# A two-layer MLP on one core: W2's block sums moved in whole blocks

## The chip, the cores and the metric

The kernel runs on one core of a Trainium2 chip. The metric is the device time of one execution in microseconds (us). A core has five engines with instruction queues of their own: TensorE (PE; its weight loads are shown as PEld), VectorE (DVE), ScalarE (ACT), GpSimd (POOL) and SyncE (SP), which here issues nearly all DMA transfers. Each queue is worked through in order; engines wait for one another by semaphores.

## The reference

```python
B, S, D, F = 1, 2048, 1024, 3584

def reference(x, w1, b1, w2, b2):
    y = _layernorm(x, axis=-1)
    h = _gelu(jnp.einsum("bsd,df->bsf", y, w1) + b1)
    return jnp.einsum("bsf,fd->bsd", h, w2) + b2
```

All inputs and the output are bf16.

## The kernel before

Both products are done by a Winograd form of Strassen's scheme: a product of 2 x 2 blocks takes seven block products of sums of blocks instead of eight. The first product (y by W1) uses it once. The second (h by W2) uses it twice: an outer level with seven products p, and inside each an inner level with seven products q. `Wino.step(q)` runs the seven and combines them in PSUM: matmuls (L878 for the first product, L1135 for the second), copies by ACT (L804, L813) and additions by DVE (L821).

Tokens come in two blocks b of 1024. x is normalised by tiles of 128 tokens; block 0's tiles are transposed by PE, block 1's by DMA transposes (L676). W1 is loaded by seven chunks of 256 columns, once for each token block (`w1_load`, L717 and L722), and its block sums are made by DVE (`w1_sums`, L745). h stays in SBUF. GELU is L797.

W2's sums are made beside the first product by the class `W2Sums`. The outer level needs, of the four blocks B11, B12, B21, B22, the sums T1 to T4; each of seven operands (B11, T1, T3, B22, B21, T2, T4, for p = 1, 5, 7, 3, 2, 6, 4) then needs four inner sums (q = 5, 6, 7, 4). W2 is taken in four chunks of k (k0 to k1 of seven: two, two, two, one). A block's chunk is held as four quarter tiles (s for the half of rows, v for the half of columns) of n = (k1 - k0) x 512 bytes a partition. `load` (L916) issues a transfer per quarter, `outer` (L927) a subtraction per quarter, `inner` (L948) makes the four sums, and `store` (L936) writes every sum, and for T1 to T4 the three quarters that q = 1, 2, 3 use, to `w2_scr` in HBM, one transfer each. In the second product `w2_unit` reads one unit of 448 KB per (p, q): from `w2_scr` (L993), or for q = 1, 2, 3 of B11, B21, B22 from W2 itself (L991). The units are used by both token blocks and loaded for the first.

Quarters and sums live in a zone of SBUF of their own, MZ, of ZONE = 20 * 1024 - 192 bytes a partition. An allocation picks the place that was freed longest ago; its first writer waits for the last readers of what lay there, DMA stores included.

The order of the work is made in two layers. `flat` is a list of steps (group, q): 73 steps of token block 0 (A, from 0), 98 of block 1 (B, from 73), 98 of the second product (C, from 171). Loads, sums and stores are put at steps of this list; a DMA put at a step is held until the PE task before that step. W2_AT spreads the 14 parts of `W2Sums.steps()` over a range of steps for each of the four chunks, and Y1_AT and Y1_STEP place the loads and norms of block 1's x tiles. Then `schedule` simulates all engines with a duration for each task, takes among the ready tasks of an engine the one that is due first, and the order that comes out is the order of each queue on the chip. For a transfer it counts an issue time (0.1 us on SP), then the transfer at 360 GB/s behind the transfers before it, and a latency (`dma_lat`). Buffers are packed by the simulated times in six rounds, and the round with the shortest simulated span is used.

Of the kernel before, what the change touches and what calls it, by code (L numbers as in the profile page):

```python
# [13 lines left out]
P = 128  # L14
# [30 lines left out]
WAR = 0.5  # L45
SLACK = 4.0
ZONE = 20 * 1024 - 192
PACK_ROUNDS = 6


# [219 lines left out]
class Program:  # L270
# [25 lines left out]
        return t  # L296


    def schedule(self, pe_t0, rounds=0, dma_bw=0.36e6, dma_lat=1.9):
        tasks = self.tasks  # L300
        for t in tasks:
            t.succ = []
        for t in tasks:
            for d in t.deps:
                d.succ.append(t)
        pe = [t for t in tasks if t.eng == "PE"]
        at = pe_t0
# [19 lines left out]
    def _simulate(self, pe, dma_bw, dma_lat):  # L327
# [17 lines left out]
        while done < len(tasks):  # L345
            progressed = False
            for e in ENG:
                q = waiting[e]
                while q and q[0][0] <= now + 1e-9:
                    _, _, t = heapq.heappop(q)  # L350
                    heapq.heappush(heaps[e], (t.alap, t.i, t))
            for e in ENG:
                h = host.get(e, e)
                while free[h] <= now + 1e-9:
                    if e == "PE":
                        if pe_next >= len(pe):
                            break
                        t = pe[pe_next]
                        if left[t] or ready_at[t] > now + 1e-9:
                            break  # L360
                        pe_next += 1
                    else:
                        if not heaps[e]:
                            break
                        _, _, t = heapq.heappop(heaps[e])
                    t.start = now
                    if e in ("SP", "ACTQ", "POOLQ"):
                        issue = 0.1 if e == "SP" else 0.5
# [12 lines left out]
                    heapq.heappush(events, t.done)  # L381
                    for s in t.succ:
                        left[s] -= 1
                        fin = t.end if (s.eng == t.eng == "PE") else t.done
                        ready_at[s] = max(ready_at[s], fin)
                        if not left[s] and s.eng != "PE":
                            heapq.heappush(waiting[s.eng], (ready_at[s], s.i, s))
                    done += 1
                    progressed = True
            if progressed:  # L390
                continue
            while events and events[0] <= now + 1e-9:
# [89 lines left out]
HEAD_T = (2, 4, 6, 7)  # L482
ACT_LN = (8, 9, 10, 11, 12, 13, 14, 15)
UNIT_LA, IN_LA = 3, 6
W2_AT = ((0, 2, ("A", 14), ("A", 50)), (2, 4, ("A", 50), ("B", 4)), (4, 6, ("B", 5), ("B", 50)), (6, 7, ("B", 50), ("C", -20)))
S1_AT = -2
W2_K = 2
NACC = 5
Y1_AT, Y1_STEP = 0, 3
T_PE = 7.5  # L490

OPA = {1: "A11", 2: "A12", 3: "S4", 4: "A22", 5: "S1", 6: "S2", 7: "S3"}
# [8 lines left out]
def d_tt(n):  # L501
    return n / 1920 + 0.075


def bass_standalone__mixer_channel_mlp__prompt_kernel(
# [24 lines left out]

    NCHUNK = NR // 2
    w1_scr = nc.dram_tensor("w1_scr", (NCHUNK, P, 4 * KH * 256), F16).ap()
    w2_scr = nc.dram_tensor("w2_scr", (8, 8, P, KQ * NCOL), F16).ap()

    with ExitStack() as es:
        block = es.enter_context(nc.Block())
# [20 lines left out]
        def build(pr, M, MA, MZ):  # L557
# [343 lines left out]
            def w2_dt(nm):  # L901
                return BF16 if nm.startswith("B") else F16

            class W2Sums:


# [2 lines left out]
                    self.B = {}  # L909

                def load(self, nm):
                    n = self.n
                    for s in range(2):
                        for v in range(2):
                            bf = self.B[nm, s, v] = MZ.alloc(n, nm)
                            dma("SP", lambda e, s=s, v=v, bf=bf: e.dma_start(v3(bf, 0, n, self.k1 - self.k0, BF16),  # L916
                                                                      w2_src(JK[nm], (s, v))[:, self.k0:self.k1, :]),
                                [], [bf.c()], P * n, None, f"ld{nm}{s}{v}")

                def outer(self, dst, a, bb, place):  # L920

                    n = self.n
                    for s in range(2):
                        for v in range(2):
                            ba, b_, bp = (self.B[z, s, v] for z in (a, bb, place))
                            op("DVE", d_tt(n // 2),
                               lambda e, ba=ba, b_=b_, bp=bp: e.tensor_tensor(out=v16(bp), in0=v16(ba, 0, n, w2_dt(a)),  # L927
                                                                             in1=v16(b_, 0, n, w2_dt(bb)), op=ALU.subtract),
                               r=[ba.c(), b_.c()], w=[bp.c()], name=f"{dst}{s}{v}")
                            self.B[dst, s, v] = self.B.pop((place, s, v))  # L930

                def store(self, p, q, buf):
                    c = Cell()
                    scr2.setdefault((p, q), []).append(c)
                    lo, hi, n = self.k0 * NCOL, self.k1 * NCOL, self.n
                    dma("SP", lambda e: e.dma_start(w2_scr[p, q][:, lo:hi], v16(buf)), [buf.c()], [c], P * n, None, f"sp2_{p}{q}")  # L936

                def inner(self, p, nm):

                    n, dt = self.n, w2_dt(nm)  # L940
                    Y = {(s, v): (v16(self.B[nm, s, v], 0, n, dt), self.B[nm, s, v].c()) for s in range(2) for v in range(2)}
                    if not nm.startswith("B"):
                        for q, sv in QIN.items():
                            self.store(p, q, self.B[nm, sv[0], sv[1]])

                    def mk(q, a, bb):
                        t = MZ.alloc(n, f"w2t{q}")
                        op("DVE", d_tt(n // 2), lambda e: e.tensor_tensor(out=v16(t), in0=a[0], in1=bb[0], op=ALU.subtract),  # L948
                           r=[a[1], bb[1]], w=[t.c()], name=f"w2t{p}{q}")
                        self.store(p, q, t)  # L950
                        return t, (v16(t), t.c())
                    b1_, t1 = mk(5, Y[0, 1], Y[0, 0])
                    b2_, t2 = mk(6, Y[1, 1], t1)
                    MZ.free(b1_)
                    b3_, t3 = mk(7, Y[1, 1], Y[0, 1])
                    MZ.free(b3_)
                    b4_, t4 = mk(4, Y[1, 0], t2)
                    MZ.free(b2_)
                    MZ.free(b4_)

                def free(self, nm):
                    for s in range(2):
                        for v in range(2):
                            MZ.free(self.B.pop((nm, s, v)))

                def steps(self):
                    return [
# [475 lines left out]
```

## Time and profile before

| | us |
|---|---|
| median of 3 runs | 384.94 |
| lowest and highest run | 384.37, 389.06 |
| the profiled execution | 383.47 |
| its span, first to last instruction | 381.5 |
| PE, DVE, ACT, POOL busy | 342.4, 299.3, 185.7, 14.9 |

The profile is of one execution. In it, L878 and the like are lines of the kernel. A row of a group names engine, operation, output and input, shapes and count, then busy us, mean ns of one, and the idle time of the engine ahead of these instructions with what ended it. `mem` is the one large SBUF tensor, `ps` a PSUM bank, `w_scr` stands for both scratch tensors in HBM, `in_w_dram` for W1 and W2. SPq is SP's queue of transfers. The slices cut the span in 40 equal parts of 9.54 us; a digit is a busy share in tenths. The DMA share is the mean busy share of the core's 16 DMA engines, from their packets' times, and can come out a little over 1.

### The profile page before, as it was taken

How to read it: one execution, taken by the hardware profiler on the slowest of the kernel's cores; microseconds unless marked ns; L12 is line 12 of the kernel's file. 1: busy time of each engine (PE TensorE's matmuls, PEld its weight loads, DVE VectorE, ACT ScalarE, POOL GpSimd, SP SyncE). 2: the span in 40 equal slices, each digit the busy share in tenths (PEclk: the TensorE clock that was granted, in tenths of full speed). 3: DMA queues.
4: the chain of work that ended last, by engine and by line, in shares of the span. 5: the costliest groups of instructions: out<-in, count | busy, mean ns of one | idle time of the engine just before them, and what ended most of it. 6: DMA issues, size and time to landing. Idle time of an engine off the chain costs nothing.

```text
span 381.5 us, 6308 instructions
## 1 busy us (share of the span) xinstructions
PE 342.4 (90%) x2363; PEld 222.6 (58%) x2363; DVE 299.3 (78%) x541; ACT 185.7 (49%) x327; POOL 14.9 (4%) x32
## 2 busy tenths in 40 slices
PE   8899987997859996799495999999999999998993
PEld 6754432443314442344142478888888888887882
DVE  4976558896788967786757799998798987799762
ACT  2598977979747663474344853444311122211110
POOL 2220000202100000000000000000000000000000
PEclk9999998999999999699698999999999999999998
DMA  8931389899986898895855255446384655567532
GB/s 246 315 103 28 97 243 273 228 278 310 253 208 206 282 310 243 285 306 176 228 157 165 64 179 151 144 144 192 112 228 147 205 157 153 184 180 220 169 121 69
DMA packets 101527, 74.01 MB, mean 194 GB/s; under 512 B 14330, under 2 KB 94330, under 8 KB 101498
## 3 DMA queue, kind: packets, MB, share of 16 engines
q1 hardware_dynamic: 101354, 73.50, 66.0%
q8 instruction: 18, 0.29, 0.3%
q10 hardware_dynamic: 144, 0.13, 0.1%
q14 instruction: 11, 0.09, 0.1%
HBM read 48.96 MB, written 22.54 MB: 187 GB/s over the span
## 4 chain that ended last, share of the span: by engine, by line
PE 60%; DMA 25%; DVE 6%; SPq 5%; issue 3%; ACT 0%; DVEq 0%
PE ps L1135 34%; PE ps L878 23%; DMA mem<-in_w_dram 15%; DMA mem<-w_scr 4%; DMA mem<-in_x_dram 3%; DMA mem<-mem 3%; SPq L916 2%; DVE mem L948 2%; PE ps L1186 2%; SPq L936 2%; DVE ps L821 1%; DVE mem L745 1%; PE ps L662 1%; DVE mem L694 1%; DVE mem L927 1%
## 5 line engine op out<-in xcount | busy, mean ns | idle before, releaser
L878 PE MATMUL ps<-mem 128*128 128x512 f16 x756 | 174.3, 391 | 27.3 <-DMA mem<-in_w_dram 17.5
L1135 PE MATMUL ps<-mem 128*128 128x256 f16 (+1 forms) x1372 | 151.7, 273 | 3.6 <-DMA mem<-in_w_dram 1.4
L878 PEld LDWEIGHTS ps<-mem 128*128 128x128 f16 (+1 forms) x756 | 74.3, 100 | 123.9 <-DMA mem<-in_w_dram 20.0
L1135 PEld LDWEIGHTS ps<-mem 128*128 128x128 f16 x1372 | 133.4, 98 | 22.5 <-DMA mem<-w_scr 2.9
L813 ACT COPY mem<-ps 128x512 f32<-128x512 f32 x111 | 65.2, 593 | 82.0 <-PE ps L1135 67.7
L797 ACT ACTIVATE mem<-ps,b_sb 128x512 f16<-128x512 f32 x112 | 73.2, 699 | 44.2 <-DVE ps L821 35.5
L1039 DVE TENSOR_TENSOR mem<-mem 128x1792 f16<-128x1792 f16 x56 | 60.3, 1085 | 11.9 <-PE ps L1135 4.7
L821 DVE TENSOR_TENSOR ps<-ps,mem 128x512 f32<-128x512 f32 x84 | 58.3, 694 | 14.3 <-ACT mem L813 9.3
L745 DVE TENSOR_TENSOR mem<-mem 128x1024 f16<-128x1024 bf16 (+1 forms) x56 | 37.0, 687 | 18.3 <-DMA mem<-in_w_dram 18.3
L948 DVE TENSOR_TENSOR mem<-mem 128x512 f16<-128x512 f16 (+3 forms) x112 | 39.8, 385 | 10.3 <-DMA mem<-in_w_dram 7.7
L804 ACT COPY ps<-ps 128x512 f32<-128x512 f32 x31 | 17.9, 579 | 35.2 <-PE ps L1135 27.8
L1050 DVE TENSOR_TENSOR mem<-mem 128x1792 f16<-128x1792 f16 x32 | 33.8, 1086 | 0.7 <-PE ps L1135 0.6
L927 DVE TENSOR_TENSOR mem<-mem 128x512 f16<-128x512 bf16 (+1 forms) x64 | 23.8, 386 | 5.9 <-DMA mem<-in_w_dram 4.0
L1067 DVE TENSOR_TENSOR mem<-ps,mem 128x512 bf16<-128x512 f32 x24 | 16.3, 689 | 8.3 <-PE ps L1135 4.2
L1080 DVE TENSOR_TENSOR mem<-ps,mem 128x512 f32<-128x512 f32 x24 | 15.9, 683 | 0.9 <-DMA out_dram<-mem 0.9
L633 DVE BATCH_NORM_STATS2 st_sb<-mem 128x6 f32<-128x512 bf16 x16 | 10.4, 672 | 5.2 <-DMA mem<-in_x_dram 5.2
L667 ACT COPY mem<-ps 128x512 f16<-128x512 f16 x16 | 8.7, 603 | 10.4 <-PE ps L662 10.4
L694 DVE TENSOR_TENSOR mem<-mem 128x512 f16<-128x512 f16 x32 | 12.0, 420 | 1.5 <-DMA mem<-mem 1.4
L616 ACT ACTIVATE mem<-mem 128x1024 f16<-128x1024 bf16 x8 | 8.4, 1052 | 4.7 <-DMA mem<-in_x_dram 4.7
L619 ACT ACTIVATE mem<-mem,mv_sb 128x1024 f16<-128x1024 bf16 x8 | 9.3, 1167 | 0.0
L1156 PE MATMUL ps<-ones 128*128 128x128 bf16 (+1 forms) x58 | 7.4, 302 | 1.0 <-POOL nhalf L583 1.0
L1186 PE MATMUL ps<-mem 128*128 128x128 f16 x112 | 7.6, 219 | 0.3 <-ACT mem L667 0.2
(30 smaller groups left out, 71.8 us busy)
## 6 DMA issues: line engine op xcount, KB each, us to landing
mem<-w_scr SPq DMA_DIRECT2D x40, 448.0 KB, 3.5
w_scr<-mem SPq DMA_DIRECT2D x120, 128.0 KB, 3.1
mem<-in_w_dram SPq DMA_DIRECT2D x28, 256.0 KB, 5.0
mem<-in_w_dram SPq DMA_DIRECT2D x14, 512.0 KB, 4.4
mem<-in_w_dram SPq DMA_DIRECT2D x48, 128.0 KB, 3.2
out_dram<-mem SPq DMA_DIRECT2D x32, 128.0 KB, 2.2
mem<-in_w_dram SPq DMA_DIRECT2D x9, 448.0 KB, 4.1
mem<-in_x_dram SPq DMA_DIRECT2D x15, 256.0 KB, 4.7
```

Source lines behind the costliest of these rows:

```text
L745: op("DVE", d_tt(n), lambda e: e.tensor_tensor(out=o[0], in0=a[0], in1=bb[0], op=f), r=[a[1], bb[1]], w=[o[1]], name=f"w1S{k}_{ch}")
L797: op("ACT", A_GELU, lambda e: e.activation(out=dst, in_=bank2(bank), func=ACT.Gelu_apprx_tanh, bias=b1_sb[:, f:f + 1], scale=1.0), r=[bank ...
L804: op("ACT", A_CP, lambda e: e.copy(out=banks[dst][:, :], in_=banks[src][:, :]), r=[bank_c[src]], w=[bank_c[dst]], name=name, lat=A_LAT)
L813: op("ACT", A_CP, lambda e: e.copy(out=v16(a, 0, 2048, F32), in_=banks[src][:, :]), r=[bank_c[src]], w=[a.c()], name=name, lat=A_LAT)
L821: op("DVE", D_PS, lambda e: e.tensor_tensor(out=banks[dst][:, :], in0=banks[src][:, :], in1=v16(a, 0, 2048, F32), op=ALU.add), r=[bank_c[s ...
L878: i = e.matmul(banks[bank][:, :], lhsT=lv[:, k, :], rhs=rv[:, k, :], start=(fresh and k == 0), stop=(k == KH - 1), skip_group_check=True)
L927: lambda e, ba=ba, b_=b_, bp=bp: e.tensor_tensor(out=v16(bp), in0=v16(ba, 0, n, w2_dt(a)), in1=v16(b_, 0, n, w2_dt(bb)), op=ALU.subtract),
L948: op("DVE", d_tt(n // 2), lambda e: e.tensor_tensor(out=v16(t), in0=a[0], in1=bb[0], op=ALU.subtract), r=[a[1], bb[1]], w=[t.c()], name=f" ...
L1039: op("DVE", d_tt(UN // 2), lambda e: e.tensor_tensor(out=v16(t), in0=a[0], in1=bb[0], op=f), r=a[1] + bb[1], w=[t.c()], name=f"in{b}_{p}{q}")
L1050: op("DVE", d_tt(UN // 2), lambda e, va=va, vb=vb, vd=vd: e.tensor_tensor(out=vd, in0=va, in1=vb, op=f), r=h_cells(b, a, u, s) + h_cells(b ...
L1067: op("DVE", D_PS, lambda e: e.tensor_tensor(out=v16(o, 0, 1024, BF16), in0=a, in1=bb, op=ALU.add), r=[na, nb], w=[o.c()], name=name, lat=D ...
L1135: i = e.matmul(bank2(bank)[:, t, :], lhsT=av3[:, k, t * P:(t + 1) * P], rhs=bv[:, k, :], start=(fresh and t == 0 and k == 0), stop=(t == 1 ...
```

## The change

A block's chunk is held as one tile of 4n bytes. `load` issues two transfers for it, one for each half of rows, with all 512 columns, so that the two column halves v lie side by side in each k. `outer` is one subtraction over the tile. `inner` makes q = 5 and 7 with one instruction (right column half minus left, and lower right minus upper right, by a view with s and v split), then 6, then 4, into one tile of four sums, which one transfer writes to `w2_scr`. For T1 to T4 one more transfer writes the whole tile, all four quarters, to a new scratch tensor `w2_raw`. `w2_unit` reads the sums from `w2_scr` at the place that POS gives, and q = 1, 2, 3 of T1 to T4 from `w2_raw` by a view that picks one column half in each k.

The simulation counts 0.5 us for an issue on any queue, and 2.2 us for `dma_lat`, where it counted 0.1 us on SP and 1.9. W2_AT moves the four chunks, in steps of the whole list, from 14 to 50, 50 to 77, 78 to 123 and 123 to 151, to 2 to 34, 36 to 68, 67 to 101 and 103 to 133. Y1_AT goes from 0 to -6; steps below 0 count as 0.

```diff
+DMA_ISSUE = 0.5
...
-    def schedule(self, pe_t0, rounds=0, dma_bw=0.36e6, dma_lat=1.9):
+    def schedule(self, pe_t0, rounds=0, dma_bw=0.36e6, dma_lat=2.2):
...
-                        issue = 0.1 if e == "SP" else 0.5
+                        issue = DMA_ISSUE
...
-W2_AT = ((0, 2, ("A", 14), ("A", 50)), (2, 4, ("A", 50), ("B", 4)), (4, 6, ("B", 5), ("B", 50)), (6, 7, ("B", 50), ("C", -20)))
+W2_AT = ((0, 2, ("A", 2), ("A", 34)), (2, 4, ("A", 36), ("A", 68)), (4, 6, ("B", -6), ("B", 28)), (6, 7, ("B", 30), ("B", 60)))
...
-Y1_AT, Y1_STEP = 0, 3
+Y1_AT, Y1_STEP = -6, 3
...
-    w2_scr = nc.dram_tensor("w2_scr", (8, 8, P, KQ * NCOL), F16).ap()
+    w2_scr = nc.dram_tensor("w2_scr", (8, 4, P, KQ * NCOL), F16).ap()
+    w2_raw = nc.dram_tensor("w2_raw", (8, P, 4 * KQ * NCOL), F16).ap()
...
+            POS = {5: 0, 7: 1, 6: 2, 4: 3}
...
                 def load(self, nm):
-                    n = self.n
+                    bf = self.B[nm] = MZ.alloc(4 * self.n, nm)
+                    j, k = JK[nm]
                     for s in range(2):
-                        for v in range(2):
-                            bf = self.B[nm, s, v] = MZ.alloc(n, nm)
-                            dma("SP", lambda e, s=s, v=v, bf=bf: e.dma_start(v3(bf, 0, n, self.k1 - self.k0, BF16),
-                                                                      w2_src(JK[nm], (s, v))[:, self.k0:self.k1, :]),
-                                [], [bf.c()], P * n, None, f"ld{nm}{s}{v}")
+                        f0 = (2 * j + s) * KQ
+                        dma("SP", lambda e, s=s, f0=f0: e.dma_start(v3(bf, 2 * s * self.n, 2 * self.n, self.k1 - self.k0, BF16),
+                                                                   w2v[:, f0 + self.k0:f0 + self.k1, k * 512:(k + 1) * 512]),
+                            [], [bf.c(s)], P * 2 * self.n, None, f"ld{nm}{s}")
...
                 def outer(self, dst, a, bb, place):
 
-                    n = self.n
-                    for s in range(2):
-                        for v in range(2):
...
+                    va, vb, vd = (v16(self.B[z], 0, 4 * self.n, dt) for z, dt in ((a, w2_dt(a)), (bb, w2_dt(bb)), (place, F16)))
+                    op("DVE", d_tt(2 * self.n), lambda e: e.tensor_tensor(out=vd, in0=va, in1=vb, op=ALU.subtract),
+                       r=self.cells(a) + self.cells(bb), w=self.cells(place), name=f"w2o{dst}")
+                    self.B[dst] = self.B.pop(place)
...
+                def inner(self, p, nm):
+
+                    n, b, dt, k = self.n, self.B[nm], w2_dt(nm), self.k1 - self.k0
+                    if not nm.startswith("B"):
+                        c = Cell()
+                        scr2.setdefault((p, "raw"), []).append(c)
+                        src = v16(b).rearrange("p (s c) -> p s c", s=2)
+                        dst = w2_raw[p].rearrange("p (s c) -> p s c", s=2)[:, :, self.k0 * 512:self.k1 * 512]
+                        dma("SP", lambda e: e.dma_start(dst, src), self.cells(nm), [c], P * 4 * n, None, f"raw{p}")
+                    y = v16(b, 0, 4 * n, dt).rearrange("p (s k v c) -> p s v k c", s=2, v=2, k=k)
+                    t = MZ.alloc(4 * n, "w2t")
+                    tv = v16(t).rearrange("p (q k c) -> p q k c", q=4, k=k)
+                    tt = lambda o, a, c: (lambda e: e.tensor_tensor(out=o, in0=a, in1=c, op=ALU.subtract))
+                    op("DVE", d_tt(n), tt(tv[:, 0:2], y[:, :, 1], y[:, 0]), r=self.cells(nm), w=[t.c(5)], name=f"w2t{p}57")
+                    op("DVE", d_tt(n // 2), tt(tv[:, 2], y[:, 1, 1], tv[:, 0]), r=[b.c(1), t.c(5)], w=[t.c(6)], name=f"w2t{p}6")
+                    op("DVE", d_tt(n // 2), tt(tv[:, 3], y[:, 1, 0], tv[:, 2]), r=[b.c(1), t.c(6)], w=[t.c(4)], name=f"w2t{p}4")
                     c = Cell()
...
+                    scr2.setdefault((p, "sum"), []).append(c)
+                    src2 = v16(t).rearrange("p (q c) -> p q c", q=4)
+                    dst2 = w2_scr[p].rearrange("q p c -> p q c")[:, :, self.k0 * NCOL:self.k1 * NCOL]
+                    dma("SP", lambda e: e.dma_start(dst2, src2), [t.c(5), t.c(6), t.c(4)], [c], P * 4 * n, None, f"sum{p}")
+                    MZ.free(t)
...
             def w2_unit(p, q):
...
-                if nm.startswith("B") and q in QIN:
-                    dma("SP", lambda e: e.dma_start(v3(bf, 0, UN, KQ, BF16), w2_src(JK[nm], QIN[q])), [], [bf.c()], P * UN, None, f"u{p}{q}")
+                if q in QIN:
+                    ss, v = QIN[q]
+                    src = w2_src(JK[nm], QIN[q]) if nm.startswith("B") else \
+                        w2_raw[p].rearrange("p (s k v c) -> p s v k c", s=2, k=KQ, v=2)[:, ss, v]
+                    dma("SP", lambda e: e.dma_start(v3(bf, 0, UN, KQ, w2_dt(nm)), src), scr2.get((p, "raw"), ()), [bf.c()], P * UN, None,
+                        f"u{p}{q}")
                 else:
-                    dma("SP", lambda e: e.dma_start(v16(bf), w2_scr[p, q]), scr2[p, q], [bf.c()], P * UN, None, f"u{p}{q}")
+                    dma("SP", lambda e: e.dma_start(v16(bf), w2_scr[p, POS[q]]), scr2[p, "sum"], [bf.c()], P * UN, None, f"u{p}{q}")
```

More of the change, by code (lines that the diff above doesn't have):

```diff
@@ L920, in outer @@
-                def outer(self, dst, a, bb, place):
-                    n = self.n
-                    for s in range(2):
-                        for v in range(2):
[L925 to L930, printed above, removed]
@@ L932, in store @@
-                def store(self, p, q, buf):
-                    c = Cell()
[L934 to L959, printed above, removed]
@@ new lines, in load, with cells @@
+                        f0 = (2 * j + s) * KQ
+                        dma("SP", lambda e, s=s, f0=f0: e.dma_start(v3(bf, 2 * s * self.n, 2 * self.n, self.k1 - self.k0, BF16),
+                                                                   w2v[:, f0 + self.k0:f0 + self.k1, k * 512:(k + 1) * 512]),
+                            [], [bf.c(s)], P * 2 * self.n, None, f"ld{nm}{s}")
+                def cells(self, nm):
+                    return [self.B[nm].c(s) for s in range(2)]
+                def outer(self, dst, a, bb, place):
+                    va, vb, vd = (v16(self.B[z], 0, 4 * self.n, dt) for z, dt in ((a, w2_dt(a)), (bb, w2_dt(bb)), (place, F16)))
+                    op("DVE", d_tt(2 * self.n), lambda e: e.tensor_tensor(out=vd, in0=va, in1=vb, op=ALU.subtract),
+                       r=self.cells(a) + self.cells(bb), w=self.cells(place), name=f"w2o{dst}")
+                    self.B[dst] = self.B.pop(place)
@@ L961, in free @@
                 def free(self, nm):
-                    for s in range(2):
-                        for v in range(2):
-                            MZ.free(self.B.pop((nm, s, v)))
+                    MZ.free(self.B.pop(nm))
                 def steps(self):
```

## The prediction

> **What bounds the kernel now.** I read the page's head first, then a table by stretches, the waits, and the timelines of SP and PE. The head: TensorE is busy nine tenths of the span, and its thin slices lie in the first 60%.
>
> ```profile
> span 381.5 us, 6308 instructions
> PE   8899987997859996799495999999999999998993
> PEclk9999998999999999699698999999999999999998
> DMA  8931389899986898895855255446384655567532
> ```
>
> The stretches below give the us, then busy us with counts in brackets of PE, PEld, DVE, ACT and POOL, the granted clock, the DMA engines' share and GB/s. At 33.8 the ordered step list ("flat") starts; its steps 0 to 170 (two token blocks of the first product) last until 218.6, then comes the second product.
>
> ```profile
> 33.80:45.00 11.20, 11.20 (x54) 4.92 (x52) 4.94 (x8) 9.67 (x18) 0.74 (x2) 1.00 0.32 96
> 45.00:154.50 109.50, 91.43 (x409) 39.33 (x406) 85.74 (x194) 78.04 (x139) 7.87 (x14) 0.98 0.90 254
> 154.50:205.50 51.00, 41.78 (x171) 17.60 (x172) 36.31 (x99) 24.80 (x42) 0.00 (x0) 0.87 0.77 230
> 218.60:381.50 162.90, 153.94 (x1384) 134.55 (x1384) 136.54 (x167) 42.15 (x73) 0.00 (x0) 0.99 0.54 162
> 33.80:218.60 184.80, 157.18 (x685) 67.30 (x682) 137.20 (x311) 121.50 (x215) 8.60 (x16) 0.94 0.78 223
> ```
>
> The stretch 33.8 to 218.6 is the one with room: PE idles 184.8 - 157.2 = 27.6 us there. What it waits for, and two timelines (start, us, then engine, line, operation, count):
>
> ```profile
> PE ps L878 <- DMA mem<-in_w_dram: 17.5, 5, 5.2
> PE ps L878 <- ACT mem L813: 5.4, 2, 3.6
> ```
> ```profile
> 148.08 0.43 SPq L722 DMA_DIRECT2D mem<-in_w_dram  x1
> 148.56 1.75 SPq L717 DMA_DIRECT2D mem<-in_w_dram  x2
> 150.35 6.95 SPq L936 DMA_DIRECT2D w_scr<-mem  x11
> ```
> ```profile
> 113.58 22.75 PE L878 MATMUL ps<-mem 128*128 128x512 f16 x104 [1.24 <-DVE mem L694]
> 154.53 26.86 PE L878 MATMUL ps<-mem 128*128 128x512 f16 x112 [4.83 <-DMA mem<-in_w_dram]
> ```
>
> Undisturbed, a matmul of L878 takes 22.75 / 104 = 0.219 us, so a step of four is 0.875 us and the 171 steps would take 149.6 us. They take 184.8: 35.2 us are the most this change can win there, 27.6 of idling and 7.6 of matmuls at a lower clock (0.87 in the stretch after 154.5, behind the gaps). The largest named cause is W1 landing late. At 154.53 PE had waited 4.83 us for a W1 load that SP issued at 148.56, though its step gates it eight steps (7 us) ahead of use.
>
> SP issues in order. Its two W2 lines (min, median and max of an issue in ns):
>
> ```profile
> L916 SPq DMA_DIRECT2D mem<-in_w_dram x64: 370/457/1344, 47.2 to 188.3; - x64
> L936 SPq DMA_DIRECT2D w_scr<-mem x160: 320/448/1753, 52.6 to 205.1; - x160
> ```
>
> 64 x 0.457 + 160 x 0.448 = 101 us of SP's queue between 47 and 205, two thirds of it, before any W1 load, x load or transpose is issued. One 128 KB transfer per 0.45 us is 290 GB/s, about what the DMA engines then move: 254 at a share of 0.90 is 282 at a full one. So two limits lie close together, the issue and the transfer, and the forecast is about which is left when the first goes.
>
> **The change, part by part.**
>
> *Transfers issued.* In four chunks of k, each chunk's 16 loads become 8, and its 40 stores become 4 raw and 7 sum stores: 32 + 16 + 28 = 76 issues for 224. At 0.45 us that is 34 us for 101, so 67 us of SP's time go. SP leaves the bound. W1 loads (and the DMA transposes) no longer stand behind eleven stores.
>
> *Bytes.* Rows: KB each, median us to landing.
>
> ```profile
> mem<-w_scr SPq DMA_DIRECT2D x40, 448.0 KB, 3.5
> w_scr<-mem SPq DMA_DIRECT2D x120, 128.0 KB, 3.1
> mem<-in_w_dram SPq DMA_DIRECT2D x14, 512.0 KB, 4.4
> mem<-in_w_dram SPq DMA_DIRECT2D x9, 448.0 KB, 4.1
> w_scr<-mem SPq DMA_DIRECT2D x40, 64.0 KB, 1.8
> ```
>
> Stores: 120 x 128 + 40 x 64 = 17,920 KB now. After: four raw products of four quarters (the quarter that no one reads goes too) and seven sums of four quarters, 44 x 448 = 19,712 KB: 1.8 MB more. Loads keep their bytes. The stretch moves 223 x 184.8 = 41.2 MB now and 43.0 after. At what rate? The lower end is 282 GB/s, from above. The upper is this one, in a piece of the same mix without transposes:
>
> ```profile
> 130.00:140.00 10.00, 9.80 (x46) 4.14 (x45) 8.98 (x21) 6.56 (x12) 0.00 (x0) 1.00 1.02 313
> ```
>
> The load rows become 1024 bytes for 512, the raw rows 2048 for 1024, the sum rows stay at 1024. No row here separates a rate by piece size, so I give that no term of its own and keep both ends.
>
> *Starting earlier.* The W2 steps move from flat 14..151 to 2..133, and block 1's x loads and norms six steps forward. In 33.8 to 45 the DMA share is only 0.32, so there is room for what is moved there. ACT has less: 9.67 of 11.2 us busy. Three tiles' norms come earlier and each is two passes of about 1.1 us: about 7 us more of ACT in that stretch if they fall there, up to 5 us of PE wait where its copies run late. Against it stands the gap of 3.6 us now (the longest of the ACT L813 row), where ACT waited for an x tile that landed late. Bounds -3.6 to +5; I take 0.
>
> *DVE.* Rows: mean ns of one.
>
> ```profile
> L1039 DVE TENSOR_TENSOR mem<-mem 128x1792 f16<-128x1792 f16 x56 | 60.3, 1085 | 11.9 <-PE ps L1135 4.7 <-DMA out_dram<-mem 3.4 <-DMA w_scr<-mem 3.1
> L745 DVE TENSOR_TENSOR mem<-mem 128x1024 f16<-128x1024 bf16 x42 | 28.3, 687 | 18.3 <-DMA mem<-in_w_dram 18.3
> L927 DVE TENSOR_TENSOR mem<-mem 128x512 f16<-128x512 bf16 x48 | 19.3, 419 | 2.3 <-DMA mem<-in_w_dram 2.0
> L927 DVE TENSOR_TENSOR mem<-mem 128x256 f16<-128x256 bf16 x16 | 4.5, 287 | 3.5 <-DMA mem<-in_w_dram 2.0 <-DMA w_scr<-mem 1.5
> L694 DVE TENSOR_TENSOR mem<-mem 128x512 f16<-128x512 f16 x32 | 12.0, 420 | 1.5 <-DMA mem<-mem 1.4
> ```
>
> 0.52 ns an element and 0.15 us an instruction. An outer is one operation of 2048 elements, 1085 + 256 x 0.52 = 1218 ns, for 4 x 419: 0.46 us less, 16 times, 7.3 us (the short chunk saves the same). An inner is 687 + 2 x 419 for 4 x 419: 0.15 us less, 28 times, 4.2 us. Its inputs are pieces of 256 elements with gaps; L694, in pieces of 128, pays nothing for that (420 beside 419). DVE's 137.2 us become 125.7. It was not the bound (L745 waited 18.3 us for W1), so I count this at nothing. The new cost, that an operation of 1.2 us may stand ahead of a PSUM addition that PE needs, is at most 0.8 us, 16 times: 13 us if every one is hit, near 0 with DVE's third of idle time. I take 0.
>
> *The second product.* The twelve units of T1 to T4 with q of 1, 2, 3 were read from w2_scr in one piece a partition (the 448 KB row, 3.5 us), and come from w2_raw in pieces of 512 bytes, as nine units of W2 itself already do (4.1 us). A load has three steps, 4.6 us, of lead. PE waited so for the two kinds:
>
> ```profile
> PE ps L1135 <- DMA mem<-in_w_dram: 1.4, 1, 1.4
> PE ps L1135 <- DMA mem<-w_scr: 1.1, 3, 0.7
> ```
>
> 1.4 / 9 = 0.16 us each for the 512-byte kind, 1.1 / 40 = 0.03 for the other: 12 x 0.13 = +1.6 us (0 to 17, if each waits 1.4). I take 1.6.
>
> *The planner.* 0.5 us per SP issue and 2.2 us of latency for 0.1 and 1.9 change only orders. A measured issue is 0.45, so its order should now hold on the chip. The gain of that lies in the 35.2 us.
>
> **The sum.** The last sums are issued by step 128, some five steps late as DVE and SP follow: step 135. By then the DMA engines must have moved 43.0 MB less the W1 of the last two chunks (2.2 MB) = 40.8 MB, from 33.8 on. At 313 GB/s that is 130 us, at 282 it is 145: step 135 falls between 164 and 178.5. The 36 steps behind it are free of W2, 31.5 us: the second product starts between 195.6 and 210, in the middle 202.8, which I take because the first half carries the transposes of the low rate and the second half not. It starts at 218.6 now: -15.8, and +1.6, is -14.2. The profiled execution took 383.47 around its span of 381.5, so 369.3. The median of the three runs is 1.47 higher; on it the forecast is 370.7, rounded to 370.
>
> Two rules of the Trainium skill bear on this. The page "DMA: Bandwidth & Descriptors", section "Issuing engines are not separate DMA queues", says that issue time is usually small beside the transfer. Here the trace disagrees: 0.45 us of issue beside 128 KB / 282 GB/s = 0.46 us of transfer. By the rule the issues saved bring nothing: the rival "transfers pace it anyway". The same page, "Queues, rings and completion order", says that each DMA engine takes its descriptors in ring order. By it a W1 load queued behind a raw and a sum store waits for 1 MB, some 3.5 us at the rates above; in the trace a 512 KB load takes 4.4 us amid 128 KB stores, and no run here shows the larger ones.
>
> **The rivals.**
>
> *All of the stall goes* (chance 0.17). If W2 may lag behind its steps without holding PE, the first product takes its 149.6 us and the second begins at 183.4: -35.2 + 1.6, so 351. For it: W2's sums are not needed before step 168. Against: DVE takes its operations in order, so a late W2 operation holds the PSUM additions behind it, and 43 MB in 149.6 us would be 287 GB/s without a pause.
>
> *The transfers pace it anyway* (0.21). At 282 GB/s or a little less, with W1 now queued behind stores four times as large, the second product starts at 210 to 219: 378 to 387, within 2%. For it: the share of 0.90 from 45 to 154.5. Against: after 154.5 the share is 0.77 with PE idling 9 us, so there it was the issue.
>
> *Slower: DVE waits for the block it writes* (0.14). MZ has 20,288 bytes. With blocks of 4096 that is four, against nineteen of 1024, and an inner's block is one whose store may still be under way. Now such waits are rare:
>
> ```profile
> DVE mem L1039 <- DMA w_scr<-mem: 3.1, 1, 3.1
> DVE mem L927 <- DMA w_scr<-mem: 1.5, 1, 1.5
> ```
>
> Two steps of W2's list, 4.6 flat steps or 4 us, lie between two uses of a block. A 512 KB transfer lands in 4.4 us, in 6.2 behind the raw store. The price is 28 waits. DVE has 125.7 us of work in the 169 us of my forecast, so it decides from (169 - 125.7) / 28 = 1.5 us a wait. At 3 us each, DVE needs 125.7 + 84 = 210 us where 184.8 are spent now: +25 + 1.6, 411. Against it: the planner sees these waits and puts other work ahead of them.
>
> **How the numbers follow.** My case has 0.48 and its own range 363 to 378. A measurement of this kernel can tell about 2%, 377.2 and 392.6. Faster than 377.2: nearly all of 0.48 and the 0.17, 0.65. Within: 0.21. Slower: 0.14. The range of 8 in 10 reaches from the full removal, 351, to the middle of the rival within 2%, 384; it leaves out the slower rival and a little at each end.
>
> **What would show it.** Right: SP issues 76 transfers on W2's lines and PE's waits for in_w_dram fall from 17.5 us to a few; the DMA share from 34 to 170 is near 1.0; the second product starts near 203; W2's outers take 1.2 us. Wrong: DVE's idle time ahead of the inner's first subtraction is put down to the stores (slower rival); PE still waits for W1 with landings of 7 us and more (transfers pace it); in the second product, waits for w_scr of over 5 us in all.

## The result and the profile after

| | us |
|---|---|
| before, median of 4 runs | 385.75 |
| after, median of 4 runs (356.57 to 357.63) | 357.29 |
| ratio after to before | 0.925, 95% interval 0.919 to 0.931 |
| the profiled execution after, its span | 357.63, 355.9 |

The forecast was 370, in a range of 351 to 384. The span fell by 25.6 us where 14.2 were forecast. Where the runs of a kernel further down lie on two levels over 1.5% apart, its ratio is formed from the lower level, none is given where that level has a single run, and its profile may be of the upper one; the runs are then given singly.

The head of the page and PE's slices, after:

```profile
span 355.9 us, 6022 instructions
...
PE   8899999979979999998996999999999999998995
...
PEclk9999999999999999999999899999999999999999
DMA  7961988999997799879996355373665737558552
```

The thin slices of PE in the first 60% are nearly gone and so is the lowered clock. The DMA digits are high from the fifth slice on, one slice earlier. In stretches (us, busy us and count of PE, PEld, DVE, ACT, POOL, granted clock, DMA share, GB/s):

```profile
33.40:45.00 11.60, 11.60 (x55) 5.15 (x54) 5.38 (x8) 10.05 (x20) 0.93 (x2) 1.00 0.88 260
...
192.90:355.90 163.00, 155.61 (x1384) 135.17 (x1384) 136.69 (x167) 41.49 (x71) 0.00 (x0) 0.99 0.55 160
...
33.40:192.90 159.50, 149.78 (x686) 65.45 (x684) 132.29 (x235) 123.74 (x216) 7.66 (x16) 1.00 0.92 272
```

Nearly all of the gain, 25.3 us, lies where the prediction looked for it: the steps of the first product took 184.8 us and take 159.5. From there to the end it is as long as it was (162.9, now 163.0). PE's idling ahead of the second product falls from 27.6 us to 9.7, and the 7.6 us of slow matmuls go with the gaps ahead of them: the clock is 1.00 throughout, and 272 matmuls in a row take 0.216 us each.

What PE waits for, in the whole span:

```profile
PE ps L1133 <- DMA mem<-w_raw: 4.2, 4, 3.0
PE ps L880 <- ACT mem L815: 2.6, 3, 2.0
PE ps L880 <- DMA mem<-in_w_dram: 2.0, 2, 1.0
PE ps L1133 <- DMA mem<-in_w_dram: 1.9, 2, 1.7
```

L880 is the first product's matmul (L878 before), L1133 the second's. The wait for W1, 17.5 us, is 2.0. A new wait stands first: 3.0 us once for w_raw. PE's timeline shows where:

```profile
105.08 58.88 PE L880 MATMUL ps<-mem 128*128 128x512 f16 x272 [1.44 <-DVE mem L696]
...
184.57 5.35 PE L880 MATMUL ps<-mem 128*128 128x512 f16 x24 [0.42 <-ACT mem L815]
192.89 1.95 PE L1133 MATMUL ps<-mem 128*128 128x256 f16 x14 [2.97 <-DMA mem<-w_raw]
```

It is the first unit of the second product, one of T4, the last sum of each chunk. The chain that ended last shows its load (start, us, what):

```profile
184.57 3.86 PE ps L880 x18
188.42 4.42 DMA mem<-w_raw
```

PE's last matmul of the first product ends at 189.9 (184.57 + 5.35). A unit is put three steps ahead of its use. Here these are steps of the first product, 2.6 us in all, so by its step the load could have gone out at 187.3. The raw store of T4 had landed by then (issued at 185.0, landed 2.4 us later). SP issued the load at 188.42, behind W2's last store at 188.0, and it took 4.42 us. So of the 2.97 us about 1.1 are the late issue, and the rest is a landing that is longer than the lead.

SP's lines for W2 (min, median, max of an issue in ns, first and last start):

```profile
L920 SPq DMA_DIRECT2D mem<-in_w_dram x32: 346/472/1247, 35.4 to 179.3; - x32
```
```profile
L942 SPq DMA_DIRECT2D w_raw<-mem x16: 513/526/1162, 44.3 to 185.0; - x16
```
```profile
L954 SPq DMA_DIRECT2D w_scr<-mem x28: 360/378/1341, 43.0 to 188.0; - x28
```

76 issues, 34 us of SP by the medians, as worked out. But the last store goes out at 188.0, right before the second product begins. By its steps it should have gone out near step 128. PE was there at about 151: by 105.08 it had run 300 matmuls, 75 steps, and 53 more take 46 us at 58.88 / 68 a step. W2's work runs 37 us behind its steps, and no wait of PE is put down to it until that first unit.

### The profile page after: what moved, and what is told of

Same layout as the page of the kernel before. It is cut to its first block, busy times and chain, and to the rows that moved or that the text cites. A ratio compares the mean times of both kernels' runs of the same rounds, so it can differ in the third digit from the quotient of the medians.

```text
span 355.9 us, 6022 instructions
## 1 busy us (share of the span) xinstructions
PE 336.5 (95%) x2363; PEld 221.4 (62%) x2363; DVE 294.6 (83%) x465; ACT 187.2 (53%) x327; POOL 13.3 (4%) x32
## 4 chain that ended last, share of the span: by engine, by line
PE 62%; DMA 23%; ACT 6%; DVE 5%; issue 3%; SPq 1%; DVEq 0%
PE ps L1133 34%; PE ps L880 26%; DMA mem<-in_w_dram 10%; DMA mem<-w_raw 7%; DMA mem<-in_x_dram 5%; ACT mem L799 2%; DVE mem L747 2%; ACT mem L815 2%; PE ps L1184 2%; DMA mem<-w_scr 1%; DVE ps L823 1%; PE ps L664 1%; DVE mem L946 1%; ACT mem L621 1%; DVE mem L696 1%
## 5 line engine op out<-in xcount | busy, mean ns | idle before, releaser
L880 PE MATMUL ps<-mem 128*128 128x512 f16 x756 | 167.6, 381 | 6.7 <-ACT mem L815 2.6
L1133 PE MATMUL ps<-mem 128*128 128x256 f16 (+1 forms) x1372 | 152.7, 273 | 7.3 <-DMA mem<-w_raw 4.2
L1133 PEld LDWEIGHTS ps<-mem 128*128 128x128 f16 x1372 | 133.8, 98 | 26.8 <-DMA mem<-w_raw 5.9
L880 PEld LDWEIGHTS ps<-mem 128*128 128x128 f16 (+1 forms) x756 | 72.5, 98 | 98.1 <-ACT mem L815 6.6
L799 ACT ACTIVATE mem<-ps,b_sb 128x512 f16<-128x512 f32 x112 | 74.2, 705 | 22.7 <-DVE ps L823 13.6
L823 DVE TENSOR_TENSOR ps<-ps,mem 128x512 f32<-128x512 f32 x84 | 58.2, 693 | 19.1 <-ACT mem L815 14.2
L946 DVE TENSOR_TENSOR mem<-mem 128x512 f16<-128x512 bf16 (+5 forms) x84 | 38.1, 464 | 10.5 <-DMA w_scr<-mem 6.9
L930 DVE TENSOR_TENSOR mem<-mem 128x2048 f16<-128x2048 bf16 (+1 forms) x16 | 17.4, 1087 | 0.2
L696 DVE TENSOR_TENSOR mem<-mem 128x512 f16<-128x512 f16 x32 | 12.0, 418 | 0.2
```

What stands on the lines that cost most here:

```text
L799: op("ACT", A_GELU, lambda e: e.activation(out=dst, in_=bank2(bank), func=ACT.Gelu_apprx_tanh, bias=b1_sb[:, f:f + 1], scale=1.0), r=[bank ...
L823: op("DVE", D_PS, lambda e: e.tensor_tensor(out=banks[dst][:, :], in0=banks[src][:, :], in1=v16(a, 0, 2048, F32), op=ALU.add), r=[bank_c[s ...
L880: i = e.matmul(banks[bank][:, :], lhsT=lv[:, k, :], rhs=rv[:, k, :], start=(fresh and k == 0), stop=(k == KH - 1), skip_group_check=True)
L930: op("DVE", d_tt(2 * self.n), lambda e: e.tensor_tensor(out=vd, in0=va, in1=vb, op=ALU.subtract), r=self.cells(a) + self.cells(bb), w=self ...
L946: tt = lambda o, a, c: (lambda e: e.tensor_tensor(out=o, in0=a, in1=c, op=ALU.subtract))
L1133: i = e.matmul(bank2(bank)[:, t, :], lhsT=av3[:, k, t * P:(t + 1) * P], rhs=bv[:, k, :], start=(fresh and t == 0 and k == 0), stop=(t == 1 ...
```

## The experiments

The change has three parts: whole blocks (with fewer issues), the planner's two numbers, and the places W2_AT and Y1_AT. My theory was that SP's issues were the limit, so that whole blocks carry the gain. The rivals: the places (using the idle transfer time from 34 us on), the planner's order, and transfers that pace it all anyway.

| parts in the kernel | us, median of 4 runs | ratio to before | 95% interval |
|---|---|---|---|
| planner | 374.23 | 0.960 | 0.951 to 0.969 |
| places | 392.39 | 1.015 | 1.010 to 1.020 |
| blocks | 373.82 | 0.966 | 0.961 to 0.972 |
| blocks, planner | 370.51 | 0.964 | 0.957 to 0.971 |
| blocks, places | 367.75 | 0.957 | 0.951 to 0.963 |
| all three | 357.29 | 0.925 | 0.919 to 0.931 |
| all three, transfers cut in pieces again | 390.62 | 1.011 | 1.006 to 1.016 |

### Transfers cut in pieces again

The nearest test of the issues: everything as after, but a half block's load is two transfers and a block's store four.

```diff
-                        dma("SP", lambda e: e.dma_start(dst, src), self.cells(nm), [c], P * 4 * n, None, f"raw{p}")
+                        for i in range(4):
+                            c = Cell()
+                            scr2.setdefault((p, "raw"), []).append(c)
+                            o = ((i // 2) * KQ + self.k0) * 512 + (i % 2) * (n // 2)
+                            dma("SP", lambda e, i=i, o=o: e.dma_start(w2_raw[p][:, o:o + n // 2], v16(b, i * n, n)), self.cells(nm), [c], P * n,
+                                None, f"raw{p}{i}")
...
-                    dma("SP", lambda e: e.dma_start(dst2, src2), [t.c(5), t.c(6), t.c(4)], [c], P * 4 * n, None, f"sum{p}")
+                    for i in range(4):
+                        c = Cell()
+                        scr2.setdefault((p, "sum"), []).append(c)
+                        dma("SP", lambda e, i=i: e.dma_start(w2_scr[p, i][:, self.k0 * NCOL:self.k1 * NCOL], v16(t, i * n, n)),
+                            [t.c(5), t.c(6), t.c(4)], [c], P * n, None, f"sum{p}{i}")
```

> The changed kernel with each load of half a block cut in two and each store of a block cut in four again: 240 issues of 64 to 128 KB for W2, the same bytes, the same vector operations, the same places, and the planner counting 0.5 us each. Issue theory: the gain goes again, 372 to 390 us, with SP's W2 issues near 105 us. If not the issues but the places, the planner or the vector operations made the gain: 355 to 363.

390.62 us, just above the range of the issue theory: the whole gain goes, and a per cent more. In its trace SP issues 64, 64 and 112 such transfers:

```profile
L927 SPq DMA_DIRECT2D mem<-in_w_dram x64: 327/432/1425, 35.1 to 205.7; - x64
```
```profile
L948 SPq DMA_DIRECT2D w_raw<-mem x64: 320/442/1569, 45.4 to 221.1; - x64
```
```profile
L960 SPq DMA_DIRECT2D w_scr<-mem x112: 319/434/1232, 41.7 to 230.1; - x112
```

That is 104.5 us by the medians, for 34. And PE's waits there (L1140 is the second product):

```profile
PE ps L1140 <- DMA mem<-w_raw: 19.4, 5, 17.7
...
PE ps L880 <- DMA mem<-in_w_dram: 3.7, 2, 3.0
```

The shortage of issues is the same as before the change, but it shows elsewhere. The planner now knows what an issue costs, puts W1 ahead, and W1's waits stay small; W2's stores are what comes late, and the second product stands 17.7 us before its first unit. The cut also makes rows of some transfers shorter, but the transfers are not what is short here:

```profile
33.50:221.40 187.90, 154.70 (x685) 66.15 (x684) 136.00 (x237) 123.53 (x215) 7.56 (x16) 0.93 0.78 224
```

The DMA engines are busy for 0.78 of the stretch, as before the change, and 224 GB/s at that share is 287 at a full one, beside 295 after (272 at 0.92). So the number of issues decides, with the planner's numbers, the places' settings and the vector operations as they are after. It also shows that the joined vector operations bring nothing while the issues are many.

### The planner alone, the places alone, the blocks alone

```diff
-    def schedule(self, pe_t0, rounds=0, dma_bw=0.36e6, dma_lat=1.9):
+    def schedule(self, pe_t0, rounds=0, dma_bw=0.36e6, dma_lat=2.2):
...
-                        issue = 0.1 if e == "SP" else 0.5
+                        issue = 0.5
```

> The kernel before with only the planner's numbers changed: 0.5 us per issue on SP and 2.2 us of latency; 224 transfers for W2 as before. Issue theory (SP's 101 us of W2 issues held W1 back): the issues remain, so 375 to 392 us, with PE's waits for in_w_dram still over 10 us. Planner theory (the order was wrong for the chip, and a true issue cost puts W1 and the transposes ahead of the stores): 357 to 368, waits for in_w_dram under 6 us.

The runs: 375.44, 373.03, 378.18, 369.24; the ratio is of 373.03 and 369.24. It gains 4% with all 224 issues, between the two expectations. The wait for W1 is halved (17.5 before), in the execution of 375.44 us:

```profile
PE ps L878 <- DMA mem<-in_w_dram: 8.5, 5, 3.2
```

So part of what I put down to the issues themselves was their order.

```diff
-W2_AT = ((0, 2, ("A", 14), ("A", 50)), (2, 4, ("A", 50), ("B", 4)), (4, 6, ("B", 5), ("B", 50)), (6, 7, ("B", 50), ("C", -20)))
+W2_AT = ((0, 2, ("A", 2), ("A", 34)), (2, 4, ("A", 36), ("A", 68)), (4, 6, ("B", -6), ("B", 28)), (6, 7, ("B", 30), ("B", 60)))
...
-Y1_AT, Y1_STEP = 0, 3
+Y1_AT, Y1_STEP = -6, 3
```

> The kernel before with only W2_AT and Y1_AT changed. Issue theory: SP is as full as before, the W2 work only starts some 11 us earlier: 376 to 390 us. Places theory (the gain comes from using the idle transfer time from 34 to 45 us): 360 to 372, with the DMA share of 34 to 45 us rising from 0.32 to over 0.8.

The transfers do start earlier (share and GB/s last; it was 0.32 and 96):

```profile
33.50:45.00 11.50, 11.50 (x55) 5.08 (x54) 6.71 (x16) 9.96 (x19) 0.84 (x2) 1.00 0.71 188
```
```profile
PE ps L878 <- DMA mem<-in_w_dram: 15.7, 5, 4.4
```

But W1's waits remain, and it is 1.5% slower, 392.39 us, above both ranges. The idle transfer time alone was of no use with 224 issues on SP and a planner that counts them at 0.1 us.

The blocks alone are the changed kernel with the two edits above undone.

> The changed kernel with the old places and the old planner numbers (0.1 us per SP issue, 1.9 us): whole blocks alone, 76 transfers for W2. Issue theory: most of the gain, 358 to 368 us. Places theory: 370 to 382. Planner theory: 372 to 390.

373.82: a gain of 3.4%, less than the issue theory's "most of it", and inside the ranges of both rivals. But its W1 waits are gone, with the old planner and the old places, and the second product waits instead:

```profile
PE ps L1133 <- DMA mem<-w_raw: 7.6, 3, 6.6
...
PE ps L880 <- DMA mem<-in_w_dram: 2.1, 3, 0.9
```

So the issues were what held W1 back, as the theory says, but freeing W1 is not yet most of the gain.

### Two of three

> The changed kernel with the old W2_AT and Y1_AT: whole blocks and the planner's new numbers, places as before. If blocks and planner act one on top of the other (0.966 and 0.960 of before), 358 us and the places add nothing. If the later places leave W2's last sums late, the second product waits for them: 363 to 372, with PE's waits for w_raw over 7 us.

> The changed kernel with the old planner numbers (0.1 us per SP issue, 1.9 us). If the planner's numbers matter only where the issues are many: 356 to 362 us. If they matter by themselves (0.960): 368 to 374.

Blocks with the planner's numbers are no better than blocks alone: 370.51 us, in the second range. With the old places W2 ends late (its last store goes out at 201.1), and PE waits 11.3 us for the first unit:

```profile
PE ps L1133 <- DMA mem<-w_raw: 12.5, 5, 11.3
```

The places then bring 0.964 down to 0.925, where alone they cost. Blocks and places without the planner's numbers stop at 0.957 (367.75 us, between the two ranges), also with a first wait for w_raw, 5.5 us. Three single ratios multiplied give 0.941; the three together reach 0.925. I read this so: the parts need one another; the issues and their order free W1, then W2's end is the limit, and only then does an earlier start count. The waits fit this, but each of these kernels is also another plan of the whole, and plans of like design differ by up to 3% further down, so no single ratio is the price of its part alone.

### Is it the transfers' rate now?

Each raw store is sent a second time, to a scratch tensor that nothing reads: 7.3 MB and only 16 issues more.

```diff
+                        two = w2_two[p].rearrange("p (s c) -> p s c", s=2)[:, :, self.k0 * 512:self.k1 * 512]
+                        dma("SP", lambda e: e.dma_start(two, src), self.cells(nm), [], P * 4 * n, None, f"two{p}")
```

> The changed kernel with each raw store of T1 to T4 sent a second time, to a scratch tensor that nothing reads: 7.3 MB and 16 issues more, all vector operations as they were. Rate theory (with the issues gone, the transfers' rate sets the pace up to the second product; 272 GB/s at a share of 0.92 is 295 at a full one, so 43.4 + 7.3 MB take 172 us for the 159.4 now): 367 to 372 us, the share over 0.95. If SP or DVE is what paces and the transfers have room: 356 to 361.

The runs: 371.32, 370.37, 363.79, 370.16. The changed kernel's program, run beside it on the same chip (the run with 290 GB/s below), took 356.89 to 357.46. Three runs are in the range of the rate theory, and 363.79 is between the two ranges. In the execution of 371.32 us the second product starts at 206:

```profile
33.50:206.00 172.50, 154.51 (x682) 66.11 (x679) 133.49 (x235) 123.71 (x214) 9.52 (x16) 0.96 0.96 292
```

172.5 us, as worked out from bytes and rate. It fits the rate theory, but no ratio can be formed, and 363.79 is only 6.3 us above the highest of 357.46. That bytes now cost time is likely; its size, and how much of it is the rate and how much the extra stores in SP's order, these runs don't show.

### W2's end, and the order of the plan

If W2's end sets the start of the second product, it should help to begin with a product whose sums are ready early:

```diff
-P_ORDER = (4, 1, 2, 6, 7, 5, 3)
+P_ORDER = (1, 4, 2, 6, 7, 5, 3)
```

> The changed kernel with the second product's outer order 1, 4, 2, 6, 7, 5, 3 for 4, 1, 2, 6, 7, 5, 3: it begins with B11, whose sums are the first of each W2 chunk, and T4, the last of all, has 21 us more. If W2's end now sets the start of the second product (PE waited 4.2 us for w_raw): 352 to 355 us, waits for w_raw under 1.5 us. If the transfers' rate sets the pace of the first product anyway: 356 to 359.

362.99 us, ratio 0.942 (0.936 to 0.948): slower than the changed kernel, against both expectations. The wait for w_raw does fall to 1.1 us, but others take its place:

```profile
PE ps L1133 <- DMA mem<-in_w_dram: 4.1, 4, 2.8
PE ps L880 <- DVE mem L696: 2.8, 1, 2.8
```

The first unit is now one of W2 itself, which needs no sum, and PE still waits 2.8 us for it:

```profile
181.07 9.86 PE ps L880 x45
190.92 5.21 DMA mem<-in_w_dram
```

Its load goes out at 190.92, as soon as its step allows, three steps of 0.86 us before PE is done with the first product, and it takes 5.2 us. So here the wait at the start of the second product is the short lead and not W2's end. The token sums of block 1 (L696) come later than they did. An edit of this kind makes the planner place everything anew, so it is not a clean test of the rest.

W2's subtractions counted as due earlier, to see whether their lag spares PE:

```diff
-                       r=self.cells(a) + self.cells(bb), w=self.cells(place), name=f"w2o{dst}")
+                       r=self.cells(a) + self.cells(bb), w=self.cells(place), name=f"w2o{dst}").eager = EAGER
```

with EAGER = 40.0, and the same on the three operations of `inner`.

> The changed kernel in which the planner counts each of W2's subtractions as due 40 us earlier, so that they go ahead of other ready work on DVE. Lag theory (the gain was larger than forecast because W2's work lags some 40 steps without holding PE): now W2 ends earlier, PSUM additions and W1 sums stand behind it, and the time goes to 362 to 375 us, with W2's last sum before 178 us. If lag is not what spared PE: 355 to 359.

365.57 us, ratio 0.949 (0.943 to 0.955), in the lag theory's range, though the last sum went out at 181, not before 178. PE's waits for W1 and for ACT's copies are many small ones, and the first unit still costs 1.7 us, though W2's last store went out 14 us before that unit's load (195.6):

```profile
PE ps L881 <- DMA mem<-in_w_dram: 4.7, 4, 2.0
PE ps L1134 <- DMA mem<-w_raw: 2.9, 3, 1.7
PE ps L881 <- ACT ps L852: 2.9, 3, 1.2
```

It fits, but as it is again another plan, it does not prove the lag theory by itself.

```diff
-                    put(i - UNIT_LA, lambda p=p, q=q: w2_unit(p, q))
+                    put(i - UNIT_LA - (q in QIN), lambda p=p, q=q: w2_unit(p, q))
```

> The changed kernel with the units of q = 1, 2, 3 of the second product put one step (1.5 us) earlier. They come in pieces of 512 bytes and PE waited 1.2 us for w_raw and 1.9 us for in_w_dram behind the first unit. If lead is what they lack: 354 to 356.5 us and those waits under 1 us together. If only the first unit counts, which stands behind W2's last store: 356.5 to 358.

The runs: 365.89, 359.79, 365.97, 365.72: above both ranges, with no ratio; 359.79 is 2.3 us above the highest of the changed kernel's program on the same chip. In the execution of 365.89 us PE's waits for w_raw and W2 behind the first unit are 0.7 us together, as the first expectation has it, but w_scr costs 2.6. The first unit's own load goes out at 196.0, 2.1 us before PE is done with the first product, and PE waits 1.7 us for it. But the largest wait of PE is one at the change of token blocks, which ends at 107.2, almost 90 us before the first unit that the edit moves:

```profile
PE ps L880 <- DVE mem L696: 5.6, 1, 5.6
...
PE ps L1133 <- DMA mem<-w_raw: 1.7, 1, 1.7
...
PE ps L1133 <- DMA mem<-in_w_dram: 0.7, 1, 0.7
```

> The changed kernel with the planner counting 290 GB/s for transfers, near what the trace shows, in place of 360. If a planner nearer to the chip gives a better order: 350 to 356 us. If the lag that the optimistic rate allows is what spares PE, or the order hardly matters now: 357 to 366.

This one was a mistake that turned into a control: `dma_bw` is handed on and read nowhere, since a transfer's duration is set at 360 GB/s where it is made. The program is the changed kernel's, and it repeats it: 357.12 us, ratio 0.925 (0.920 to 0.930). The rate was then changed in the right place (`nbytes / 0.36e6` to `nbytes / 0.29e6`):

> The changed kernel with the duration of a transfer counted at 290 GB/s where the transfers are made (the parameter of the run before is read nowhere, so that run repeated the changed kernel's program). If a plan at the chip's rate is the better one: 350 to 356 us, with PE's waits ahead of the second product under 6 us. If its order is only another one of similar worth: 357 to 367, as for the kernels with another lead and another outer order.

368.52 us, ratio 0.952 (0.946 to 0.958): worse than both expectations. Here the plan lets W2 end later and the token sums too:

```profile
PE ps L1133 <- DMA mem<-w_raw: 10.7, 3, 10.1
PE ps L880 <- DVE mem L696: 6.3, 1, 6.3
```

A truer rate in the plan did not give a better order. No kernel tried here beats the changed one.

## Why the prediction was right, and where its size was off

**The bound before: right in kind.** SP's issues held W1 back: with whole blocks alone W1's waits fall from 17.5 to 2.1 us, and cutting the transfers again takes the whole gain away (1.011). What the prediction missed is that the order counts too: the planner's numbers alone are worth 4%. It had put them inside the 35.2 us without a share.

**Issues and bytes: right.** 76 issues and 34 us; 272 GB/s over 159.5 us is 43.4 MB, for 43.0. (W1 of two chunks is twice 1,024 KB, 2.1 MB and not 2.2; that moves the sum by 0.4 us at most.)

**The rate: inside its bounds.** 272 at a share of 0.92 is 295 GB/s at a full one, between 282 and 313.

**The failed term: "the 36 steps behind it are free of W2, 31.5 us".** The sum let W2 end at step 135 and then added 36 steps of PE. It took for granted that a late W2 holds PE back. In the trace W2's last store goes out at 188.0, with PE at its last steps of the first product, and the second product starts 4.9 us later. In PE's terms the 192.9 are 149.8 us of matmuls and 9.7 of idling from 33.4 on, for the 202.8 forecast: 9.9 of the 11.4 us that the span is shorter than forecast. "All of the stall goes" had this right: W2 may lag. What kept it from its 183.4 is mostly not W2's end. 6.7 of the 9.7 us are small waits of the first product (ACT's copies 2.6, W1 2.0, token sums 1.4, and smaller ones), and of the 3.0 for the first unit about 1.1 are W2's last store. The prediction gave a unit's load three steps, 4.6 us, of lead; for the first unit these are steps of the first product, 2.6 us, beside a landing of 4.4. Made after the fact, the sum of bytes comes out too: 43 MB from 33.8 on at the low rate take 152.5 us, to 186, near the last store. So transfers and PE end close together here, and no run parts the two.

**The number.** 357.29 lies outside the 363 to 378 of my own case, and nearer to the 351 of "All of the stall goes", to which I had given 0.17. The range held because it reached down to that rival.

**The second product: the other 1.5 us, by chance.** +1.6 forecast, +0.1 measured, but not because the +1.6 was wrong. Behind the first unit PE's waits for units rise from 1.8 us (W2 1.4, w_scr 0.4) to 3.5 (w_raw 1.2, W2 1.9, w_scr 0.4). From its first matmul to its last the second product takes 159.9 us for 156.9; what these waits leave of the 3.0 are slower matmuls behind the wait for the first unit. Against this stands the tail behind PE's last matmul, 5.6 us before and 3.1 now. The last work of PE before and after, and the addition that made the old tail long by waiting for a store of outputs:

```profile
372.63 3.23 PE L1135 MATMUL ps<-mem 128*128 128x256 f16 x28 [0.68 <-ACT mem L813]
...
378.45 0.69 DVE L1067 TENSOR_TENSOR mem<-ps,mem 128x512 bf16<-128x512 f32 x1 [1.87 <-DMA out_dram<-mem]
```
```profile
349.60 3.23 PE L1133 MATMUL ps<-mem 128*128 128x256 f16 x28 [0.68 <-ACT mem L815]
```

**DVE: counted at nothing, and smaller than worked out.** An outer takes what was estimated:

```profile
L930 DVE TENSOR_TENSOR mem<-mem 128x2048 f16<-128x2048 bf16 x12 | 14.7, 1221 | 0.2
```

1221 ns for 1218. But W2's two lines fell only from 63.6 us (39.8 and 23.8) to 55.5 (38.1 and 17.4), 8.1 for 11.5, and all of DVE's work in the steps of the first product from 137.2 to 132.3, where 125.7 was worked out.

**The slower rival: its wait is there and small.**

```profile
DVE mem L946 <- DMA w_scr<-mem: 6.9, 6, 3.3
```

6 of 28 inners waited for the store of their block, 0.25 us an inner over all, where the rival needed 1.5.

**The two rules.** That issue time is usually small beside the transfer (the Trainium skill, "DMA: Bandwidth & Descriptors", "Issuing engines are not separate DMA queues") does not hold for this kernel's 128 KB transfers: their number, with bytes and vector operations the same, moves the ratio from 0.925 to 1.011. The ring order of the same page ("Queues, rings and completion order") would have put some 3.5 us on a W1 load behind two large stores. Measured, the median of a 512 KB load went from 4.4 to 5.0 us:

```profile
mem<-in_w_dram SPq DMA_DIRECT2D x14, 512.0 KB, 5.0
```

So the trace shows a small part of it; how many stores stood ahead of each load was not followed.

**What stays open.** Why plans of similar design differ by 3 to 10 us; part of the changed kernel's 357 may be a lucky plan, and no run shows how much. In the profiled executions of three of the slower ones (another lead, another rate, raw stores twice) a wait of 5.3 to 6.3 us for block 1's token sums appears (1.4 in the changed kernel), behind transfers at a share of 0.95 to 1.02 up to 105 us. The share there is 0.99 in the changed kernel too; which transfer is late was not followed.

## What to carry to other kernels

Count the issues of a queue by their measured time before the bytes: here 0.45 us an issue made 128 KB transfers as slow to hand out as to move, and the work that suffered was not the one that issued them but a load that stood behind it. When such a limit goes, ask what the freed work is due for: it need not end where its steps are placed (here it ran 37 us late and cost about 1 us). And count a lead in the steps that lie ahead of that load: three steps were 4.6 us inside the second product and 2.6 ahead of it. Parts of a change can need one another; the places cost 1.5% alone and gained 4% on top of the other two.

## What had not been expected of the hardware

An issue on SP does not follow the bytes: the median of the sum stores of 256 to 512 KB is 0.38 us (L954), that of the raw stores of the same sizes 0.53 (L942), and that of stores of 64 to 128 KB 0.45 (L936 before). And VectorE's rows overlap: before the change the 112 subtractions of `inner` have a mean of 385 ns, 43.1 us in all, but were busy 39.8 us. Added up, the durations of W2's two lines fell by 11.4 us (67.8 to 56.4), as worked out; but short operations back to back cost less than their durations added up, so joining them gained 8.1 us in these lines.

A wait of PE also shows in the matmuls behind it. The first 14 of the second product take 1.70 us behind a wait of 0.69 (before) or 2.00 (raw stores twice), 1.95 behind 2.97 (after), and 3.17 behind 5.50 (blocks and places):

```profile
201.40 3.17 PE L1133 MATMUL ps<-mem 128*128 128x256 f16 x14 [5.50 <-DMA mem<-w_raw]
```
